# A gated layer in 64-row tiles and two phases in place of full-height tiles

## The chip, the cores and the metric

The kernel runs on one core of a Trainium2 chip. The metric is device time in microseconds (us), lower is better. Five engines work side by side, each on its own queue in program order: PE (matrix multiplies into PSUM banks), ScalarE (ACT), VectorE (DVE), GpSimd (POOL) and SyncE (SP, which issues loads). They wait for one another through semaphores.

## What is computed

Three layers run one after the other: a gated linear attention, an expert layer in which each of 3,072 tokens passes one of eight experts, and a gated layer over all tokens. The change lies in the third, whose reference is:

```python
def _moe2_ref(x, w_gate, w_val, w_out):
    gate = 1.0 / (1.0 + np.exp(-(x @ w_gate)))
    val = x @ w_val
    return (gate * val @ w_out).astype(np.float32)
```

Here x has 3,072 rows and 320 columns, w_gate and w_val are 320 by 1,536, w_out is 1,536 by 320. The weights come in 64 bits. To keep 32-bit accuracy every factor is split in a high and a low part of a shorter format (float32r), and a product is the sum of three: high·high, high·low, low·high.

## The kernel before, in words

The gated layer works on six groups g of 512 tokens and twelve tiles f of 128 hidden columns: 72 steps (g, f), in the order `order2` (line 1451). A step t of the loop at line 1599 does the following.

- `piece_due` and `piece` (lines 1472 and 1465): the weights are loaded in pieces of 320 or 384 columns and split from 64 bits by `f64_split` (line 1060): three DVE operations, an ACT Relu, two or more DVE operations that need it, and an ACT cast. Some pieces are split in the expert layer already, 19 in the first 18 or so steps. `todo` (line 1454) holds each piece with the step at which it is due.
- `gated_l1(t)` (line 1530): PE computes the gate tile g_ps and the value tile v_ps, each 128 hidden columns by 512 tokens in one PSUM bank out of four (0, 1, 2, 6). `l1_tile` (line 916) contracts over 320 rows: two blocks of 128 rows with three products each, then the last 64 rows. For these the tile wgs (or wvs) holds the high part of the weights in rows 0 to 63 and the low part in rows 64 to 127, and x has its last 64 rows twice; so two full-height products are enough, at the price of a fourth product (low·low) that is not needed. In all 8 products for each tile, 16 per step. Then ACT takes the sigmoid of g_ps, DVE multiplies by v_ps, ACT casts the result to the high part hh, POOL subtracts to get the low part hl.
- `gated_l2(t - 2)` (line 1551): the second layer, two steps late. For each of four blocks of 128 tokens three products with w_out (320 columns) into output banks 3, 4, 5 and 7: 12 products. At the end of a group the banks are copied (`gated_keep`, `gated_out`).
- `group_x` (line 1480) on some steps: ACT and POOL split the tokens of the next group.

After the loop the last two steps' second layers are computed block by block (line 1614), each with its output transfer. The program's own order is kept (a manual schedule): what stands here is each engine's queue.

Of the kernel before, what the change touches and what calls it, by code (L numbers as in the profile page):

```python
# [15 lines left out]
ALU = mybir.AluOpType  # L16
# [6 lines left out]
def kernel(  # L23
# [1171 lines left out]
    def flag_ops():  # L1195
# [14 lines left out]
        def of_expert(u):  # L1210
# [23 lines left out]
            lambda: v.tensor_tensor(out=fb, in0=z(0), in1=z(1), op=ALU.add),  # L1234
            total,
# [3 lines left out]
            lambda: v.tensor_tensor(out=z(2), in0=ps[0][:, 0:1], in1=z(2), op=ALU.add),  # L1239
            lambda: v.tensor_scalar_min(z(2), z(2), 1.0),  # L1240
# [171 lines left out]
    for nm in ("wg", "wv"):  # L1412
        glu[nm] = (
            gp.tile([P, 2, F2], F32R, name=nm + "h"),
            gp.tile([P, 2, F2], F32R, name=nm + "l"),
            gp.tile([P, F2], F32R, name=nm + "s"),
        )

    def whole(t):
        return t  # L1420

    def glu_piece(nm, kk, c0, n):
        cs = slice(c0, c0 + n)
        if kk < 2:
            src = (w_gate if nm == "wg" else w_val)[:, cs].bitcast(I32)
            hi, lo, st = glu[nm]
# [3 lines left out]
        halves = [slice(u * RM, (u + 1) * RM) for u in range(2)]  # L1430
# [4 lines left out]
        def parts(u):  # L1435
            return [
                (lambda z, r=r: z[r], glu[m][2][halves[u], cs]) for r, m in zip(halves, ("wg", "wv"))
            ]

        return lambda: f64_split(t, n, parts(0), parts(1))  # L1440

# [81 lines left out]
    todo += [(when[f] + 2, lambda f=f: wo_load(f)) for f in range(NF2)]  # L1523
    todo.sort(key=lambda z: z[0])
# [4 lines left out]

    def gated_l1(t):  # L1530
        g, f = order2[t]
        pg, pv = (next_bank((0, 1, 2, 6), nm) for nm in ("g_ps", "v_ps"))
        l1_tile(pg, glu["wg"], xg[g], f)
        l1_tile(pv, glu["wv"], xg[g], f)
        s = mw.tile([P, NM], F32, tag="sgm", bufs=2, name="sgm")
        nc.scalar.activation(out=s, in_=pg, func=AF.Sigmoid)  # L1536
        nc.vector.tensor_tensor(out=s, in0=pv, in1=s, op=ALU.mult)  # L1537
        gh, gl = ring("hh"), ring("hl")
        nc.scalar.copy(gh, s)  # L1539
        e = nc.gpsimd if t < last else nc.vector  # L1540
        e.tensor_tensor(out=gl, in0=s, in1=gh, op=ALU.subtract)  # L1541
        hs[t] = (gh, gl)

    def begins(t):
        g, f = order2[t]
        return f == 0 or (g < 2 and f == NH)

    def ends_(t):
        return t == last or begins(t + 1)

    def gated_l2(t, js):
# [45 lines left out]
    xsteps.update({order2.index((1, 6)) + 2 * u: (2, u) for u in range(3)})  # L1597
    xsteps.update({order2.index((g, 4 + 2 * u)): (g + 1, u) for g in range(2, NG - 1) for u in range(3)})
    for t in range(NG * NF2):
# [12 lines left out]
        if t in xsteps:  # L1612
            group_x(*xsteps[t])
# [190 lines left out]
    NSB = NE * NTILE  # L1804

    def more_blocks(fp):
        gw = fp.tile([P, NTILE], F32, name="gw")
# [52 lines left out]
        with tc.For_i(0, NE, 1) as e:  # L1860
# [6 lines left out]
            with tc.If(high > low):  # L1867
# [7 lines left out]
                with tc.For_i(low, high, 1) as j:  # L1875
# [36 lines left out]
                    for f in range(NF2):  # L1912
                        pg = mm_ps("fg_ps")[:, 0:P]
                        l1_tile(pg, glu["wg"], (yh, yl), f)
                        pv = mm_ps("fv_ps")[:, 0:P]
                        l1_tile(pv, glu["wv"], (yh, yl), f)
# [71 lines left out]
```

## Time and profile before

| | us |
|---|---|
| median of 3 runs | 773.56 (772.23 to 776.41) |
| the profiled execution's own time | 772.58 |
| its span (first to last instruction) | 770.9 |
| PE busy | 737.4, 96% of the span |
| DVE, ACT, POOL busy | 408.8, 340.0, 393.3 |
| first matmul of the gated layer | 372.3 after the span's start |
| start of its last step | 753.06 |

A matmul group's "busy" is a union of pipelined instructions, whose ends are modelled; what counts is the time from one start to the next. The profile has the granted clock of PE as a share of full speed: 1.00 is 2.4 GHz, 0.50 is 1.2 GHz. "PEld" is PE's weight load. In a row of the timeline "[2.24 <-PE g_ps L926]" says that the engine sat idle 2.24 us before it and what ended that.

### The profile page before, as it was taken

What the parts mean: (1) busy time and instruction counts of PE and PEld (TensorE: products, weight loads), DVE (VectorE), ACT (ScalarE), POOL (GpSimd) and SP (SyncE); (2) the same over time, 40 slices, a digit from 0 to 9 for tenths busy, and PEclk for the clock granted to TensorE, in tenths of its full rate; (3) what the DMA queues carried; (4) which work ended last, traced back from release to release, by engine and by line L of the source; (5) the groups of instructions that cost most, each with busy time, mean ns of one, the idle gap of its engine ahead of it and who ended that gap; (6) DMA issues with size and microseconds to landing.
All of it is one profiled execution on the core that took longest, in us unless ns stands there. A gap on an engine that the chain in (4) does not pass through costs nothing. (4 is left out here: it accounts for less than half of the span.)

```text
span 770.9 us, 13685 instructions
## 1 busy us (share of the span) xinstructions
PE 737.4 (96%) x5013; PEld 667.9 (87%) x5013; DVE 408.8 (53%) x866; ACT 340.0 (44%) x689; POOL 393.3 (51%) x449
## 2 busy tenths in 40 slices
PE   6789998999999999999999999999999999999995
PEld 5689998899878989999888888888888888888885
DVE  7888888878579787855577775121121111111111
ACT  5766554544866655765444343222222222222221
POOL 6677777547676767886242224443334324324222
PEclk9999999599999999999999999999999999999998
DMA  7644765445545566551122221000000000000001
GB/s 224 193 154 148 233 201 153 135 127 150 165 133 157 142 194 180 167 173 58 35 72 80 67 64 34 19 35 0 1 10 27 1 0 35 1 1 34 1 1 38
DMA packets 39846, 70.19 MB, mean 91 GB/s; under 512 B 4818, under 2 KB 28460, under 8 KB 39772
## 3 DMA queue, kind: packets, MB, share of 16 engines
q1 hardware_dynamic: 36764, 59.61, 26.3%
q0 software_dynamic: 3008, 9.64, 3.9%
q8 instruction: 41, 0.67, 0.4%
q14 instruction: 33, 0.27, 0.1%
HBM read 60.55 MB, written 8.68 MB: 90 GB/s over the span
## 5 line engine op out<-in xcount | busy, mean ns | idle before, releaser
L1541 POOL TENSOR_TENSOR hl<-sgm,hh 128x512 fp32r<-128x512 f32 x71 | 91.9, 1294 | 245.1 <-ACT hh L1539 245.1
L1537 DVE TENSOR_TENSOR sgm<-v_ps,sgm 128x512 f32<-128x512 f32 x72 | 49.8, 692 | 244.8 <-PE v_ps L926 244.3
L1539 ACT CAST hh<-sgm 128x512 fp32r<-128x512 f32 x72 | 44.7, 621 | 132.5 <-DVE sgm L1537 132.5
L1536 ACT ACTIVATE sgm<-g_ps 128x512 f32<-128x512 f32 x72 | 42.9, 596 | 109.1 <-PE g_ps L926 109.0
L1561 PE MATMUL o_ps<-wo,hh 128*128 128x320 f32 x288 | 89.0, 309 | 0.0
L1562 PE MATMUL o_ps<-wo,hl 128*128 128x320 f32 x288 | 89.0, 309 | 0.0
L1560 PE MATMUL o_ps<-wo,hh 128*128 128x320 f32 x288 | 88.6, 308 | 0.0
L1014 ACT ACTIVATE hh<-h_ps 128x256 fp32r<-128x256 f32 (+7 forms) x72 | 35.2, 489 | 56.4 <-PE h_ps L926 53.1
L429 PE MATMUL s_ps<-qk 128*128 128x128 f32 (+1 forms) x384 | 52.4, 298 | 6.5 <-DMA qk<-in_qkt_dram 6.5
L1561 PEld LDWEIGHTS o_ps<-wo,hh 128*128 128x128 f32 x288 | 54.0, 188 | 3.1 <-DVE wo L1071 0.4
L1560 PEld LDWEIGHTS o_ps<-wo,hh 128*128 128x128 f32 x288 | 54.1, 188 | 2.7
L1015 DVE SCALAR_TENSOR_TENSOR hl<-h_ps,hh 128x256 fp32r<-128x256 f32 (+7 forms) x72 | 39.5, 551 | 30.9 <-ACT hh L1014 30.5
L429 PEld LDWEIGHTS s_ps<-qk 128*128 128x128 f32 (+1 forms) x384 | 47.7, 206 | 7.6 <-DMA qk<-in_qkt_dram 4.5
L1562 PEld LDWEIGHTS o_ps<-wo,hl 128*128 128x128 f32 x288 | 54.1, 188 | 0.0
L223 POOL TENSOR_TENSOR w1l<-w1raw,w1h 128x512 fp32r<-128x512 f32 x32 | 44.4, 1386 | 14.2 <-ACT w1h L220 12.5
L922 PE MATMUL h_ps<-xh,w1h 128*128 128x256 f32 (+7 forms) x144 | 50.9, 354 | 0.0
L935 PE MATMUL y_ps<-hh,w2h 128*128 128x256 f32 (+7 forms) x144 | 50.0, 347 | 0.0
L936 PE MATMUL y_ps<-hl,w2h 128*128 128x256 f32 (+7 forms) x144 | 48.8, 339 | 0.8 <-DVE hl L1015 0.8
L924 PE MATMUL h_ps<-xh,w1l 128*128 128x256 f32 (+7 forms) x144 | 49.2, 342 | 0.0
L923 PE MATMUL h_ps<-xl,w1h 128*128 128x256 f32 (+7 forms) x144 | 49.1, 341 | 0.0
L234 POOL TENSOR_TENSOR w2l<-w2raw,w2h 128x512 fp32r<-128x512 f32 x28 | 36.8, 1316 | 23.6 <-ACT w2h L232 18.7
L937 PE MATMUL y_ps<-hh,w2l 128*128 128x256 f32 (+7 forms) x144 | 48.7, 338 | 0.0
(337 smaller groups left out, 2081.6 us busy)
## 6 DMA issues: line engine op xcount, KB each, us to landing
kv<-in_kvo_dram SPq DMA_DIRECT2D x24, 484.0 KB
w2raw<-in_moe_w_dram SPq DMA_DIRECT2D x32, 320.0 KB
w1raw<-in_moe_w_dram SPq DMA_DIRECT2D x32, 256.0 KB
qk<-in_qkt_dram SPq DMA_DIRECT2D x48, 160.0 KB
xs<-x SPq DMA_DIRECT2D x24, 192.0 KB
w1raw<-in_moe_w_dram SPq DMA_DIRECT2D x64, 64.0 KB
raw<-in_moe_w_out_dram SPq DMA_DIRECT2D x12, 320.0 KB
raw<-in_moe_w_gate_dram SPq DMA_DIRECT2D x8, 384.0 KB
```

Of the source, the lines that this page charges most:

```text
L429: nc.tensor.matmul(pss[u][:, pr_ * L:(pr_ + 1) * L], qk[i % NQ][rows, 2 * u, pr_, :], qk[i % NQ][rows, 1, pr_, :], start=True, stop=True,)
L922: nc.tensor.matmul(ps, hi[:, kk, fs], h[:, kk], start=(kk == 0), stop=False)
L923: nc.tensor.matmul(ps, hi[:, kk, fs], l[:, kk], start=False, stop=False)
L924: nc.tensor.matmul(ps, lo[:, kk, fs], h[:, kk], start=False, stop=False)
L935: nc.tensor.matmul(ys[d], wh, hh, start=first, stop=False)
L936: nc.tensor.matmul(ys[d], wh, hl, start=False, stop=False)
L937: nc.tensor.matmul(ys[d], wl, hh, start=False, stop=last)
L1537: nc.vector.tensor_tensor(out=s, in0=pv, in1=s, op=ALU.mult)
L1541: e.tensor_tensor(out=gl, in0=s, in1=gh, op=ALU.subtract)
L1560: nc.tensor.matmul(o, gh[:, ts_], wh, start=begins(t), stop=False)
L1561: nc.tensor.matmul(o, gh[:, ts_], wl, start=False, stop=False)
L1562: nc.tensor.matmul(o, gl[:, ts_], wh, start=False, stop=ends_(t))
```

## The change

All products of the gated layer are cut into 64-row halves; PE addresses the rows 0 to 63 and the rows 64 to 127 as two tiles, with weights of their own, and a product of one half and one of the other are issued in turn.

- The first layer is in two phases. `gated_a`: the three products of the last 64 rows (the tiles wth and wtl hold the gate's in rows 0 to 63 and the value's in rows 64 to 127), then for both 128-row blocks the lower half of the rows into g_ps and the upper half into v_ps. `gated_b`: the lower half into v_ps and the upper into g_ps.
- The second layer (`gated_l2h`) has two phases in the same way: in the first the lower half of hh and hl goes into one output bank and the upper half into its neighbour, in the second the other way round.
- The two halves are kept from writing one bank at the same time: `note` has ACT write one element after a phase's last product, and `turn_rows` has the next phase's first product wait for that write.
- A step is now: phase one of the first layer, phase one of the second layer of step t-2, phase two of the first, phase two of the second. A piece's split is cut in three: its middle stands before phase two, its casts behind it, its first DVE operations after the step's DVE product.
- Phase one of steps 0 and 1 and a whole piece (the first of w_out) come before phase two of step 0. Pieces are due one step earlier.
- The last 64 rows' pieces need one cast and one DVE operation less each. In the last step the operations between the layers are cut in two column halves. The one-column product of the flags is issued together with its reader.

```diff
-    todo = [(when[z[2] // P], lambda z=z: glu_piece(*z)) for z in todo]
+    todo = [(when[z[2] // P] - 1, lambda z=z: glu_piece(*z)) for z in todo]
...
+    def products(rows, ps, w, x, kk, fs, start=False, stop=False):
+        (wh, wl), (h, l) = w, x
+        at = lambda z: z[rows, kk, fs] if len(z.shape) == 3 else z[rows, fs]
+        return [
+            lambda: nc.tensor.matmul(ps, at(wh), h[rows, kk], start=start, stop=False),
+            lambda: nc.tensor.matmul(ps, at(wh), l[rows, kk], start=False, stop=False),
+            lambda: nc.tensor.matmul(ps, at(wl), h[rows, kk], start=False, stop=stop),
+        ]
...
+    def note(ins, key):
+
+        passed[key] = nc.scalar.copy(seen, zeros[0:1, 0:1])
+        tc.add_manual_dep(passed[key].ins, ins.ins.name, sync, reason="these products are done")
+
+    def turn_rows(ins, key):
+
+        tc.add_manual_dep(ins.ins, passed.pop(key).ins.name, sync, reason="the other rows wrote the bank")
+
-    def gated_l1(t):
+    def gated_a(t):
         g, f = order2[t]
-        pg, pv = (next_bank((0, 1, 2, 6), nm) for nm in ("g_ps", "v_ps"))
-        l1_tile(pg, glu["wg"], xg[g], f)
-        l1_tile(pv, glu["wv"], xg[g], f)
+        fs = slice(f * P, (f + 1) * P)
+        gv[t] = [next_bank((0, 1, 2, 6), nm) for nm in ("g_ps", "v_ps")]
+        weave(*(products(r, ps, tails, xg[g], 2, fs, start=True) for r, ps in zip(halves, gv[t])))
+        for kk in range(2):
+            ins = woven(*(products(r, ps, w, xg[g], kk, fs) for r, ps, w in zip(halves, gv[t], gate_val)))
+        note(ins[-1], "l1")
+
+    def gated_b(t):
+        g, f = order2[t]
+        fs = slice(f * P, (f + 1) * P)
+        for kk in range(2):
+            ins = woven(*(
+                products(r, ps, w, xg[g], kk, fs, stop=(kk == 1))
+                for r, ps, w in zip(halves, gv[t][::-1], gate_val[::-1])
+            ))
+            if kk == 0 and "l1" in passed:
+                turn_rows(ins[0], "l1")
...
+    def gated_l2h(t, phase):
...
+        for j in (0, 2):
+            ins = woven(*(three(halves[u], j + (u ^ swap)) for u in range(2)))
+            if phase and j == 0:
+                turn_rows(ins[0], "l2")
+        if not phase:
+            note(ins[-1], "l2")
...
     for t in range(NG * NF2):
-        g, f = order2[t]
         piece_due(t)
-        gated_l1(t)
+        if t == 0:
+            gated_a(0)
+            gated_a(1)
+            for ops in piece():
+                weave(ops)
         if t >= 2:
-            gated_l2(t - 2, allj)
+            gated_a(t)
+            gated_l2h(t - 2, 0)
+        weave(rest[0])
+        weave(rest[1])
+        s = gated_b(t)
+        if t >= 2:
+            gated_l2h(t - 2, 1)
             if ends_(t - 2):
                 g2, f2 = order2[t - 2]
                 (gated_out(g2, allj) if f2 == NF2 - 1 else gated_keep(g2))
-        weave(defer[0:2], *piece())
+        weave(rest[2])
+        a, *rest = piece()
+        weave(a)
+        gated_h(t, s)
+        weave(defer[0:2])
```

How the order moves. First PE's queue in a step. Before, the end of the first layer and the first two blocks of the second (g_ps, v_ps: gate and value; o_ps: output banks; wo: w_out; waits on an engine's semaphore in brackets):

```order
L925 MATMUL v_ps<-xg,wvs 128x512
L926 MATMUL v_ps<-xg,wvs 128x512
L1560 MATMUL o_ps<-wo,hh 128x320 [waits Activation_49]
L1561 MATMUL o_ps<-wo,hh 128x320 [waits DVE_49]
L1562 MATMUL o_ps<-wo,hl 128x320 [waits Pool_49]
L1560 MATMUL o_ps<-wo,hh 128x320
```

Now, the end of phase one, phase one of the second layer (two blocks of tokens in each run of rows marked x2) and the start of phase two:

```order
L1533 MATMUL g_ps<-xg,wgl 128x512
L1533 MATMUL v_ps<-xg,wvl 128x512
L1609 MATMUL o_ps<-wo,hh 128x320 x2
L1610 MATMUL o_ps<-wo,hh 128x320 x2
L1611 MATMUL o_ps<-wo,hl 128x320 [waits Pool_49]
L1611 MATMUL o_ps<-wo,hl 128x320
L1609 MATMUL o_ps<-wo,hh 128x320 x2
L1610 MATMUL o_ps<-wo,hh 128x320 x2
L1611 MATMUL o_ps<-wo,hl 128x320 x2
L1531 MATMUL v_ps<-xg,wvh 128x512 [waits Activation_49]
L1531 MATMUL g_ps<-xg,wgh 128x512
```

The second layer, which was one run of 12 products behind the first, now stands in two halves, and the first of them lies between the two phases of the first layer. Phase two begins with a wait for ACT.

Second, ACT's queue from the end of the expert layer on. Before (sgm: the sigmoid's tile; fa and fb: a piece's; wo: a piece of w_out; xh: tokens of the next group):

```order
L968 COPY yT_3227<-y_ps_5075 128x336 [waits Pool_49]
L1536 ACT_TABLE_LOAD
L1536 ACTIVATE sgm_5265<-g_ps_5247 128x512 [waits PE_49]
L1539 CAST hh_5268<-sgm_5265 128x512 [waits DVE_49]
L1085 ACTIVATE fa_5272<-fa_5272,relu_b_2322 128x320 [waits DVE_49]
L1068 CAST wo_5239<-fb_5273 128x320 [waits DVE_49]
L1536 ACTIVATE sgm_5303<-g_ps_5285 128x512 [waits PE_49,Activation_49]
L1539 CAST hh_5306<-sgm_5303 128x512 [waits DVE_49]
L1085 ACTIVATE fa_5310<-fa_5310,relu_b_2322 128x320 [waits DVE_49]
L1068 CAST wo_5239<-fb_5311 128x320 [waits DVE_49]
L209 CAST xh_5323<-yT_3227 128x512 [waits Activation_49]
```

Now, from the write that follows phase one of step 1:

```order
L1545 COPY seen_5243<-zeros_94 1x1 [waits PE_49,Activation_49]
L1085 ACTIVATE fa_5286<-fa_5286,relu_b_2322 128x320 [waits DVE_49]
L1068 CAST wo_5235<-fb_5287 128x320 [waits DVE_49]
L1574 ACT_TABLE_LOAD
L1574 ACTIVATE sgm_5311<-g_ps_5244 128x512 [waits PE_49]
L1585 CAST hh_5320<-sgm_5311 128x512 [waits DVE_49]
L1085 ACTIVATE fa_5314<-fa_5314,relu_b_2322 128x320 [waits DVE_49]
L1574 ACTIVATE sgm_5342<-g_ps_5265 128x512 [waits PE_49]
L1068 CAST wo_5235<-fb_5315 128x320 [waits DVE_49]
L1585 CAST hh_5352<-sgm_5342 128x512 [waits DVE_49]
L209 CAST xh_5356<-yT_3227 128x512
L1545 COPY seen_5243<-zeros_94 1x1 [waits PE_49,Activation_49] x2
```

The writes into `seen` come ahead of everything else; the first piece's Relu and cast moved ahead of the table load and of the first sigmoid, and the writes for step 2 (the last row) stand behind two steps' sigmoids and casts and a cast of tokens.

## Rows read from the trace of the kernel before

**Rows 1.** Stage table: stretch, each engine's busy us, clock, DMA share, GB/s.

```profile
379.60:500.00 120.40, 120.35 (x623) 105.60 (x622) 74.39 (x144) 49.74 (x95) 42.04 (x33) 1.00 0.20 56
```

**Rows 2.** Timeline, two steps of the gated layer, PE: start us, us, engine.

```profile
520.43 0.39 PE L922 MATMUL g_ps<-xg,wgh 128*128 128x512 f32 x1
520.43 0.19 PEld L923 LDWEIGHTS g_ps<-xg,wgh 128*128 128x128 f32 x1
523.85 0.39 PE L926 MATMUL v_ps<-xg,wvs 128*128 128x512 f32 x1
524.08 0.30 PE L1560 MATMUL o_ps<-wo,hh 128*128 128x320 f32 x1
525.83 0.39 PE L922 MATMUL g_ps<-xg,wgh 128*128 128x512 f32 x1
```

**Rows 3.** The same timeline, ScalarE and VectorE in that step.

```profile
522.52 0.60 ACT L1536 ACTIVATE sgm<-g_ps 128x512 f32<-128x512 f32 x1 [2.24 <-PE g_ps L926]
524.35 0.69 DVE L1537 TENSOR_TENSOR sgm<-v_ps,sgm 128x512 f32<-128x512 f32 x1 [4.44 <-PE v_ps L926]
525.07 0.62 ACT L1539 CAST hh<-sgm 128x512 fp32r<-128x512 f32 x1 [1.95 <-DVE sgm L1537]
```

**Rows 4.** Timeline of the first score products, 40 rows each, then full-height ones.

```profile
4.97 0.58 PE L429 MATMUL s_ps<-qk 40*128 40x128 f32 x2 [0.31 <-DMA qk<-in_qkt_dram]
4.97 0.29 PEld L429 LDWEIGHTS s_ps<-qk 40*128 40x128 f32 x2 [0.60 <-DMA qk<-in_qkt_dram]
4.97 2.07 PE L429 MATMUL s_ps<-qk 40*128 40x128 f32 x14 [0.31 <-DMA qk<-in_qkt_dram]
10.84 3.48 PE L429 MATMUL s_ps<-qk 128*128 128x128 f32 x15 [2.28 <-DMA qk<-in_qkt_dram]
```

**Rows 5.** Groups of instructions, ScalarE, whole span: count, busy us, mean ns.

```profile
L1397 ACT ACTIVATE dum<-zeros 128x1 f32<-128x1 f32 x1 | 0.2, 203 | 0.0
L209 ACT CAST xh<-yT 128x512 fp32r<-128x512 f32 x9 | 5.5, 616 | 0.0
```

**Rows 6.** Timeline, start of the gated layer, and one later piece (446.55).

```profile
372.29 0.39 PE L922 MATMUL g_ps<-xg,wgh 128*128 128x512 f32 x1
373.40 1.28 ACT L1536 ACT_TABLE_LOAD   x1
377.46 0.56 ACT L1085 ACTIVATE fa<-fa,relu_b 128x320 int32<-128x320 int32 x1
377.63 1.29 POOL L1541 TENSOR_TENSOR hl<-sgm,hh 128x512 fp32r<-128x512 f32 x1 [10.88 <-ACT hh L1539]
378.05 1.22 DVE L1086 SCALAR_TENSOR_TENSOR fb<-raw,fa 128x320 int32<-128x320 int32 x1 [0.92 <-ACT fa L1085]
379.30 0.46 ACT L1068 CAST wo<-fb 128x320 fp32r<-128x320 f32 x1 [1.28 <-DVE fb L1086]
380.18 0.49 DVE L1071 SCALAR_TENSOR_TENSOR wo<-fc,fa 128x320 fp32r<-128x320 int32 x1
446.55 0.56 DVE L1086 SCALAR_TENSOR_TENSOR fb<-raw,fa 128x384 int32<-128x384 int32 x1 [0.68 <-ACT fa L1085]
```

**Rows 7.** Timeline, a ScalarE result that PE's weight load waits for.

```profile
20.25 0.62 ACT L483 ACTIVATE cst<-u_ps 40x164 f32<-40x164 f32 x2
20.92 0.20 PEld L476 LDWEIGHTS u_ps<-vw,kv 128*40 128x40 f32 x6 [0.96 <-ACT cst L483]
```

**Rows 8.** Stage table: two stretches with little PE work, and those behind them.

```profile
31.20:34.60 3.40, 2.19 (x30) 1.98 (x31) 2.79 (x9) 2.95 (x9) 3.27 (x7) 1.00 0.83 224
34.60:38.00 3.40, 3.40 (x19) 3.40 (x18) 3.15 (x4) 1.97 (x7) 1.88 (x2) 0.50 0.96 308
133.60:137.00 3.40, 1.11 (x7) 0.60 (x7) 2.66 (x5) 1.19 (x3) 2.02 (x4) 1.00 0.97 302
137.00:157.50 20.50, 20.06 (x139) 19.66 (x139) 15.51 (x45) 10.96 (x30) 12.30 (x16) 0.50 0.45 134
```

**Rows 9.** Timeline, the last step's subtraction on VectorE.

```profile
758.36 0.69 DVE L1541 TENSOR_TENSOR hl<-sgm,hh 128x512 fp32r<-128x512 f32 x1 [0.69 <-ACT hh L1539]
```

More of the change, by code (lines that the diff above doesn't have):

```diff
@@ L1238, in flag_ops @@
             ),
[L1239 removed]
+            lambda: (total(), v.tensor_tensor(out=z(2), in0=ps[0][:, 0:1], in1=z(2), op=ALU.add)),
             lambda: v.tensor_scalar_min(z(2), z(2), 1.0),
@@ L1415 @@
             gp.tile([P, 2, F2], F32R, name=nm + "l"),
-            gp.tile([P, F2], F32R, name=nm + "s"),
         )
+    tails = [gp.tile([P, F2], F32R, name="wt" + v) for v in "hl"]
     def whole(t):
         return t
+    halves = [slice(u * RM, (u + 1) * RM) for u in range(2)]
     def glu_piece(nm, kk, c0, n):
@@ L1425, in glu_piece @@
             src = (w_gate if nm == "wg" else w_val)[:, cs].bitcast(I32)
-            hi, lo, st = glu[nm]
+            hi, lo = glu[nm]
             t = f64_load([(slice(0, P), src[kk * P:(kk + 1) * P])], n)
             return lambda: f64_split(t, n, [(whole, hi[:, kk, cs])], [(whole, lo[:, kk, cs])])
-        halves = [slice(u * RM, (u + 1) * RM) for u in range(2)]
         t = f64_load(
@@ L1433, in glu_piece @@
         )
[L1435 to L1440, printed above, removed]
+        return lambda: f64_split(t, n, [(whole, tails[0][:, cs])], [(whole, tails[1][:, cs])])
     todo = sorted(
@@ L1522 @@
     load_wo()
-    todo += [(when[f] + 2, lambda f=f: wo_load(f)) for f in range(NF2)]
+    todo += [(when[f] + 1, lambda f=f: wo_load(f)) for f in range(NF2)]
     todo.sort(key=lambda z: z[0])
@@ L1528 @@
     hs, os_ = {}, {}
-    def gated_l1(t):
-        g, f = order2[t]
-        pg, pv = (next_bank((0, 1, 2, 6), nm) for nm in ("g_ps", "v_ps"))
-        l1_tile(pg, glu["wg"], xg[g], f)
-        l1_tile(pv, glu["wv"], xg[g], f)
-        s = mw.tile([P, NM], F32, tag="sgm", bufs=2, name="sgm")
-        nc.scalar.activation(out=s, in_=pg, func=AF.Sigmoid)
-        nc.vector.tensor_tensor(out=s, in0=pv, in1=s, op=ALU.mult)
+    gv = {}
+    gate_val = (glu["wg"], glu["wv"])
+    def products(rows, ps, w, x, kk, fs, start=False, stop=False):
[6 more added lines that the diff above has]
+        ]
@@ new lines, with woven @@
+    seen = const.tile([1, 1], F32, name="seen")
+    sync = mybir.DependencyInfo(mybir.DependencyClass.Sync, mybir.DependencyReason.DATA)
+    passed = {}
+    def woven(*chains):
+        return [op() for ops in zip(*chains) for op in ops]
+    def note(ins, key):
[3 more added lines that the diff above has]
+        tc.add_manual_dep(ins.ins, passed.pop(key).ins.name, sync, reason="the other rows wrote the bank")
@@ new lines, in gated_a @@
+    def gated_a(t):
+        g, f = order2[t]
+        fs = slice(f * P, (f + 1) * P)
[14 more added lines that the diff above has]
+                turn_rows(ins[0], "l1")
+        pg, pv = gv.pop(t)
+        s = mw.tile([P, NM], F32, tag="sgm", bufs=2, name="sgm")
+        for cs in col_parts(t):
+            nc.scalar.activation(out=s[:, cs], in_=pg[:, cs], func=AF.Sigmoid)
+            nc.vector.tensor_tensor(out=s[:, cs], in0=pv[:, cs], in1=s[:, cs], op=ALU.mult)
+        return s
@@ L1538, in gated_l1, with col_parts, gated_h @@
+    def col_parts(t):
+        return [slice(0, NM)] if t < last else [slice(u * NM // 2, (u + 1) * NM // 2) for u in range(2)]
+    def gated_h(t, s):
         gh, gl = ring("hh"), ring("hl")
-        nc.scalar.copy(gh, s)
         e = nc.gpsimd if t < last else nc.vector
-        e.tensor_tensor(out=gl, in0=s, in1=gh, op=ALU.subtract)
+        for cs in col_parts(t):
+            nc.scalar.copy(gh[:, cs], s[:, cs])
+            e.tensor_tensor(out=gl[:, cs], in0=s[:, cs], in1=gh[:, cs], op=ALU.subtract)
@@ L1549, in ends_, with three @@
         return t == last or begins(t + 1)
+    def gated_l2h(t, phase):
+        g, f = order2[t]
+        swap = (f + phase) % 2
+        begin, end = begins(t) and phase == 0, ends_(t) and phase == 1
+        if begin:
+            os_[g] = [bank(j, "o_ps") for j in (3, 4, 5, 7)]
+        gh, gl = hs[t]
+        wh, wl = wo[f]
+        def three(rows, j):
+            o = os_[g][j][:, 0:DM]
+            ts_ = slice(j * P, (j + 1) * P)
+            return [
+                lambda: nc.tensor.matmul(o, gh[rows, ts_], wh[rows], start=begin, stop=False),
+                lambda: nc.tensor.matmul(o, gh[rows, ts_], wl[rows], start=False, stop=False),
+                lambda: nc.tensor.matmul(o, gl[rows, ts_], wh[rows], start=False, stop=end),
+            ]
+        for j in (0, 2):
[4 more added lines that the diff above has]
+            note(ins[-1], "l2")
     def gated_l2(t, js):
@@ L1598 @@
     xsteps.update({order2.index((g, 4 + 2 * u)): (g + 1, u) for g in range(2, NG - 1) for u in range(3)})
+    rest = ([],) * 3
     for t in range(NG * NF2):
-        g, f = order2[t]
         piece_due(t)
-        gated_l1(t)
-        if t >= 2:
-            gated_l2(t - 2, allj)
+        if t == 0:
[3 more added lines that the diff above has]
+                weave(ops)
+        if t >= 2:
+            gated_a(t)
[5 more added lines that the diff above has]
+            gated_l2h(t - 2, 1)
             if ends_(t - 2):
@@ L1804, with l1_any @@
     NSB = NE * NTILE
+    def l1_any(ps, u, x, f):
+        fs = slice(f * P, (f + 1) * P)
+        for rows, w, kk in (
+            (slice(0, P), gate_val[u], 0), (slice(0, P), gate_val[u], 1), (halves[u], tails, 2)
+        ):
+            weave(products(rows, ps, w, x, kk, fs, start=(kk == 0), stop=(kk == 2)))
     def more_blocks(fp):
```

5 lines of the change are left out of this document (2 added, 3 removed).

## The prediction

> **What bounds the kernel now.** I read the stage table first. In the gated layer the matrix engine (PE) is busy 120.35 of 120.40 us [rows 1], so this phase is worth exactly what PE's own work in it is worth. Next, the timeline of one step: its first matmul starts at 520.43, the next step's at 525.83, a period of 5.40 us [rows 2]. The 16 products of 512 columns fill 520.43 to 524.08, 0.228 us each (I use 0.227, the pitch inside the run), and the 12 of 320 columns fill 524.08 to 525.83, 0.146 us each. The difference, 0.081 us for 192 columns, is 2.4 columns per ns; so 512 columns stream in 0.213 us, 320 in 0.133, and every matmul carries a fixed 13 ns besides. The weight load of the next matmul starts with the matmul before it and lasts 0.19 us [rows 2]: it is hidden. The other engines' work of a step is a chain of 0.60, 0.69, 0.62 and 1.29 us [rows 3, 6], far below 5.40, and PE never waits for it. The page's chain of what ended last holds only the final output transfer and says nothing of this phase.
>
> **What the change removes.** The 64 tail rows of the contraction cost each of the two tiles g and v two full-height products (hi and lo of the weights stacked in one tile): 4 slots of 512 per step. They become three products of 64 rows each for g and v, and g's and v's run side by side, one in each half of the rows: 3 slots. All other products are cut in two 64-row halves, which also run side by side, so their slots stay: 12 of 512 and 12 of 320. Per step 15 slots of 512 in place of 16: one slot of 0.227 us, over 72 steps **−16.3 us**. This rests on two claims.
>
> First, do halves run at the same time? The trace has 64-row tiles in one place: the first 16 score products, 40 rows each in alternate halves. A pair of them takes 0.58 us together, and its two weight loads 0.29 [rows 4]: partners start side by side, within 0.01 us as the row can tell. Fourteen of them take 2.07 us, while 15 full-height ones of the same 128 columns soon after take 3.48 [rows 4]. Less 0.58 us for one, that is 0.115 us for each further half product against 0.207 for a full one, though not all of the fourteen met a partner. So they overlap, loads included.
>
> Second, what does a pair cost at 512 and 320 columns? Fixed rest and partners' offset decide. No row shows it at these sizes. Best case: the partners hide each other's 13 ns, the pair is 0.213. Worst case with overlap: each pays its own, 0.240. I take one rest per pair, 0.227 and 0.146, because the pairs of [rows 4] show no pitch of their own beside that of full-height products. The Trainium skill has a rule that speaks against this change. In "TensorEngine Tiling (Array Packing)", Performance Considerations, each matmul has an overhead of about 60 cycles; an estimate from it, 25 ns at 2.4 GHz for each of the 26 matmuls added to 28, is 0.65 us per step or +47 us, against +0 by my sum. The 13 ns of [rows 2] disagree with it as a price in a stream.
>
> **What it adds.** Two one-element ScalarE (ACT) writes per step, 0.20 us each [rows 5], each waited for by PE. In the steady step let e be the end of phase two of the first layer. PE then has 6 slots of 320 (to e+0.88), phase one of the next step (9 slots, e+2.92) and 6 slots of 320 (e+3.80) before it needs the first write. A result reaches another engine 0.27 us after its slot (matmul at 523.85, slot over at 524.08, VectorE (DVE) at 524.35 [rows 2, 3]); ACT's writes reach PE's load within 0.05 us (20.87 to 20.92 [rows 7]), and I allow 0.10. So the write may run e+3.19 to e+3.39 and PE may go on at e+3.49, 0.31 us early: nothing is lost, the cover being the 0.88 us of output products. ACT must be free at e+3.19; sigmoid, DVE's product and the cast end by e+2.25, with a group's cast of 0.62 by e+2.87. The second write has phase two, 1.36 us, as cover. Behind a late write ACT's next sigmoid is queued, and DVE's product and GpSimd (POOL) behind that; none is near its limit.
>
> In the first 18 steps DVE also splits weight pieces, now cut in three parts around the step. The long operation of a piece took 1.22 us while POOL subtracted, and 0.56 when POOL was idle (446.55) [rows 6]. Now it comes after POOL's subtraction, so it gets shorter; DVE's product is late by some 0.1 us and the cover holds. I charge 0.6 us for small waits here and at the copies of output banks, which PE now needs sooner after they were filled.
>
> **The start is where it loses.** All of ACT's queue stands behind the two first writes (order, above). By hand, from the durations of [rows 3, 5, 6]: PE starts at 372.29; phase one of steps 0 and 1 is 18 slots, to 376.37. The second write runs 376.64 to 376.84 and PE goes on at 376.94: 0.6 us lost, with nothing between to cover it. Only now come the piece's Relu (to 377.40), DVE's long operation (378.0), the cast (378.5), the table load of 1.28 (379.8), sigmoid (380.4) and DVE's product (381.1). PE has finished both phases two at 379.7, and phase one of step 2 needs the bank that this product reads: 1.5 us lost. Then cast, Relu, sigmoid of step 1 (382.9), DVE's piece, held up by POOL until 383.4, its product (384.9), cast and the group's cast (386.2) stand ahead of the write that step 2 waits for: it ends at 386.4, PE was through at 384.1: 2.4 us lost. Sum **+4.5 us**. Before, the table load ran at 373.40 to 374.68, hidden.
>
> **The clock.** After stretches in which PE was busy 2.19 of 3.40 us and 1.11 of 3.40 us the granted clock was 0.50 for 3.4 and for 20.5 us [rows 8]. From 379.7 to 386.5 PE would be busy 2.9 of 6.8 us, so I expect one such fall. Half speed for 3.4 us loses 1.7, for 20.5 us 10.2. I take **+1.7**, as the row with the shorter fall had PE busy all through, as here.
>
> **The end.** The last step's chain, split in column halves, is covered by 6+3 slots of 320 where it had 12+3. With halves it takes about 1.5 us (half an activation, product and cast, each near 0.4) after a cover of 1.3: +0.4; before, the subtraction began at 758.36 [rows 9] under running products. Dropped tail copies and the moved one-column product lie beside PE's work: 0. SP has only the piece loads, due a step later: 0.
>
> Sum: −16.3 + 4.5 + 0.6 + 1.7 + 0.4 = −9.1. The profiled execution took 772.6 us; that gives **763.5**. The median shown, 773.56, is 1.0 above that execution. About 0.5% (3.9 us) is what a measurement can tell from no change.
>
> **The rivals.**
> *A rest per matmul (slower).* If the 13 ns belong to an engine-wide step, each of the 54 matmuls pays them: 27 × 13.3 ns × 72 = +25.9, **789.4**. It decides from 4.7 ns per pair on (9.1 us over 1,944 pairs). For it: the rest is there at both sizes. Against: the pairs of [rows 4]. Chance 0.11.
> *The partners' offset adds up (no change).* The two of [rows 4] bound it by 10 ns; at half that, 5 ns × 1,944 = +9.7, **773.2**. The Trainium skill's page "TensorE: Matmul & The Clock Gate", Part 3 (Packing small matmuls), gives about 4 ns per further tile; by it the estimate is +7.8, 771.3. Chance 0.10.
> *The rest is hidden in the pair.* −25.9, **737.6**; half of it 750.5. For it: two loads overlapped fully. Chance 0.12.
> *Overlap fails at full speed.* The pairs of [rows 4] ran at 0.21 us per 128 columns, slow ones. If none overlaps, 5.16 us per step more, 1,135. The same Part 3 of the Trainium skill states a speedup of 3.07 for four tiles; an estimate with that share of the ideal is a pair 1.3 times as long, some 110 us more. Chance 0.04.
> *The waits are dearer.* The write's cover fails by 0.1 us in each step (+7), or the clock stays low for 20 us (+8.5): **771**. Chance 0.06.
>
> **How the numbers follow.** My case, 0.57, spans 757 to 771: start loss 2 to 6, clock 0 to 10. With the offset case, the dearer waits and the better half of the hidden rest down to 749, and up to 779, about 0.78 is held. Faster: 0.53 of my case and 0.12, so 0.65; same: 0.04, 0.10 and 0.03, so 0.17; slower 0.18.
>
> **What would show it.** Right: a steady step of 5.16 to 5.20 us; partners starting within 0.01 us; next pair 0.227 and 0.146 later; no wait of PE for the one-element writes after step 3; three waits near 377, 380 and 385 us, the granted clock perhaps at 0.50 behind them. Wrong: pair pitches other than these, a wait on the write in every step, a table load that hides, or PE idle for long at the last step.

## The result, and the profile after

The changed kernel takes 767.39 us (median of 7 runs, 764.88 to 769.53) against 773.75 for the kernel before in the same comparison: a ratio of 0.991, 95% interval 0.990 to 0.9925. The forecast was 763.5, faster; the time lies 3.9 us above it, inside the range of 757 to 771.

The profiled execution took 767.39 us, its span is 765.6 (before: 772.6 and 770.9). From the first product of the gated layer to the span's end it is 391.7 us where it was 398.6: 6.9 us gained. Ahead of the gated layer, where the change does no more than shorten the splitting of some weight pieces, this execution is 1.6 us longer (the first product starts at 373.87, before at 372.29 [rows 6]). Its first spell of half clock lasts 6.8 us where that of [rows 8] lasts 3.4, which is the likely reason; no run isolates it.

The stage table of the changed kernel (stretch, its length, then busy us and instructions of PE, PEld, DVE, ACT and POOL, then clock, DMA share, GB/s). First the stretch of that spell, then two of the gated layer:

```profile
31.20:34.60 3.40, 2.11 (x9) 1.78 (x9) 2.87 (x9) 2.95 (x9) 3.27 (x6) 0.62 0.92 301
379.60:500.00 120.40, 117.83 (x1200) 101.45 (x1198) 66.88 (x142) 57.59 (x138) 44.67 (x33) 1.00 0.20 57
500.00:620.00 120.00, 120.00 (x1237) 104.22 (x1235) 25.43 (x56) 40.57 (x100) 45.08 (x37) 1.00 0.03 12
```

PE is still the bound; the 2.6 us in which it idles in the second stretch ([rows 1] had 0.05) are the start of the layer. Its timeline, PE, ScalarE and VectorE (start, us, engine):

```profile
378.69 0.50 PE L1531 MATMUL v_ps<-xg,wvh 64*128 64x512 f32 x1 [0.34 <-ACT seen L1545]
380.14 1.28 ACT L1574 ACT_TABLE_LOAD   x1
382.06 0.69 DVE L1575 TENSOR_TENSOR sgm<-v_ps,sgm 128x512 f32<-128x512 f32 x1 [1.55 <-ACT sgm L1574]
382.08 0.50 PE L1531 MATMUL g_ps<-xg,wth 64*128 64x512 f32 x1 [0.33 <-ACT sgm L1574]
382.81 0.49 PE L1531 MATMUL v_ps<-xg,wth 64*128 64x512 f32 x1 [0.23 <-DVE sgm L1575]
386.78 0.62 ACT L1585 CAST hh<-sgm 128x512 fp32r<-128x512 f32 x1 [1.03 <-DVE sgm L1575]
387.82 0.41 ACT L1545 COPY seen<-zeros 1x1 f32<-1x1 f32 x2
388.06 0.50 PE L1531 MATMUL v_ps<-xg,wvh 64*128 64x512 f32 x1 [2.01 <-ACT seen L1545]
390.44 0.39 PE L1531 MATMUL g_ps<-xg,wth 64*128 64x512 f32 x1
```

These are the three waits of the forecast, each with the releaser it named: the write behind step 1 (378.69), sigmoid and product behind the table load (382.08, 382.81), the writes behind the cast of step 1 (388.06). Step 3 begins at 390.44, 16.57 us after the first product. In the kernel before it began here, 12.66 us after the first product:

```profile
384.95 0.39 PE L922 MATMUL g_ps<-xg,wgh 128*128 128x512 f32 x1
```

With the 0.5 us that the three steps save in slots, the start loses 4.4 us.

A step in the middle, PE and ScalarE of the changed kernel:

```profile
521.72 0.39 PE L1531 MATMUL g_ps<-xg,wth 64*128 64x512 f32 x1
521.72 0.39 PE L1531 MATMUL v_ps<-xg,wth 64*128 64x512 f32 x1
523.81 0.31 PE L1609 MATMUL o_ps<-wo,hh 64*128 64x320 f32 x2
524.07 0.19 ACT L1545 COPY seen<-zeros 1x1 f32<-1x1 f32 x1 [0.98 <-PE v_ps L1533]
524.69 0.39 PE L1531 MATMUL v_ps<-xg,wvh 64*128 64x512 f32 x1
526.09 0.30 PE L1609 MATMUL o_ps<-wo,hh 64*128 64x320 f32 x2
526.96 0.39 PE L1531 MATMUL g_ps<-xg,wth 64*128 64x512 f32 x1
```

Partners start together. The period is 5.24 us (526.96 less 521.72), where it was 5.40 to 5.41 [rows 2] and 5.16 to 5.20 was forecast. The 12 pairs of 320 columns take 0.88 and 0.87 us, as full products did. But the nine pairs of 512 columns take 2.09 (521.72 to 523.81), the six 1.40: 0.233 us a pair, not 0.227. The write ends at 524.26; PE goes on at 524.69, right behind the products of w_out, and has not waited.

### The profile page after: what moved, and what is told of

Read it like the earlier page. It is cut to its first block, busy times and chain, and to the rows that moved or that the text cites. A ratio compares the mean times of both kernels' runs of the same rounds, so it can differ in the third digit from the quotient of the medians.

```text
span 765.6 us, 17594 instructions
## 1 busy us (share of the span) xinstructions
PE 730.9 (95%) x6861; PEld 656.2 (86%) x6861; DVE 402.4 (53%) x864; ACT 363.9 (48%) x829; POOL 395.5 (52%) x449
## 5 line engine op out<-in xcount | busy, mean ns | idle before, releaser
L1611 PE MATMUL o_ps<-wo,hl 64*128 64x320 f32 x560 | 87.2, 307 | 0.0
L1610 PE MATMUL o_ps<-wo,hh 64*128 64x320 f32 x560 | 86.7, 305 | 0.0
L1609 PE MATMUL o_ps<-wo,hh 64*128 64x320 f32 x560 | 86.3, 303 | 0.0
L1531 PE MATMUL v_ps<-xg,wvh 64*128 64x512 f32 x144 | 56.5, 392 | 2.4 <-ACT seen L1545 2.4
L1609 PEld LDWEIGHTS o_ps<-wo,hh 64*128 64x128 f32 x560 | 53.0, 185 | 6.3
L1610 PEld LDWEIGHTS o_ps<-wo,hh 64*128 64x128 f32 x560 | 52.8, 184 | 5.8
L1531 PE MATMUL g_ps<-xg,wgh 64*128 64x512 f32 x144 | 56.5, 392 | 0.0
L1532 PE MATMUL v_ps<-xg,wvh 64*128 64x512 f32 x144 | 56.4, 392 | 0.0
L1532 PE MATMUL g_ps<-xg,wgh 64*128 64x512 f32 x144 | 56.4, 392 | 0.0
L1532 PE MATMUL g_ps<-xl,wgh 64*128 64x512 f32 x144 | 56.4, 392 | 0.0
L1532 PE MATMUL v_ps<-xl,wvh 64*128 64x512 f32 x144 | 56.4, 392 | 0.0
L1531 PE MATMUL g_ps<-xh,wgh 64*128 64x512 f32 x144 | 56.3, 391 | 0.0
L1531 PE MATMUL v_ps<-xh,wvh 64*128 64x512 f32 x144 | 56.3, 391 | 0.0
L1533 PE MATMUL g_ps<-xg,wgl 64*128 64x512 f32 x144 | 56.2, 390 | 0.0
```

Of the source, the lines that this page charges most:

```text
L1531: lambda: nc.tensor.matmul(ps, at(wh), h[rows, kk], start=start, stop=False),
L1532: lambda: nc.tensor.matmul(ps, at(wh), l[rows, kk], start=False, stop=False),
L1533: lambda: nc.tensor.matmul(ps, at(wl), h[rows, kk], start=False, stop=stop),
L1609: lambda: nc.tensor.matmul(o, gh[rows, ts_], wh[rows], start=begin, stop=False),
L1610: lambda: nc.tensor.matmul(o, gh[rows, ts_], wl[rows], start=False, stop=False),
L1611: lambda: nc.tensor.matmul(o, gl[rows, ts_], wh[rows], start=False, stop=end),
```

## Experiments

A ratio is that of a run's time to the kernel before, measured beside it. A step, or the gated layer's part (from its first product to the span's end), is read from the run's trace. A slot is the time from the start of one product, or pair, to the start of the next; a turn is a change between full-height products and halves.

**1. Only the tail in halves.** The order of before, 12 full products, then three pairs:

```
for ps, w in zip(pss, gate_val):
    for kk in range(2):
        weave(products(slice(0, P), ps, w, xg[g], kk, fs, start=(kk == 0)))
weave(*(products(r, ps, tails, xg[g], 2, fs, stop=True) for r, ps in zip(halves, pss)))
```

> Only the tail rows are done in halves: 3 pairs of 64-row products for g and v together; the other 12 products of 512 columns and the 12 of 320 are full-height again, in the order of the kernel before, without phases and without the one-element writes. A step is then 12 x 226.7 + 3 x 233 + 12 x 146.7 ns = 5.18 us, if going from full products to halves and back costs nothing. Theory: each such turn costs 0.20 us. In the trace of the changed kernel the slot before the first pair of the gated layer lasts 0.247 in place of 0.153 us and that pair's own 0.340 in place of 0.233; at the end, where full products follow halves, 0.239 and 0.253 in place of 0.147 each. Two turns a step, 72 steps: +28.8 us, about 788 us, a step of 5.58. Rival: those stretched slots are waits of that place, and a turn in the middle of a stream is free: 759 us, a step of 5.18 to 5.20, and the phases and writes of the change were not needed.

Measured: 790.13 us, ratio 1.021 (1.019 to 1.023), a step of 5.64. Its timeline at the two turns, PE:

```profile
525.39 0.39 PE L1533 MATMUL v_ps<-xg,wvl 128*128 128x512 f32 x1
525.72 0.50 PE L1531 MATMUL g_ps<-xg,wth 64*128 64x512 f32 x1
526.06 0.39 PE L1532 MATMUL g_ps<-xg,wth 64*128 64x512 f32 x1
526.29 0.39 PE L1533 MATMUL g_ps<-xg,wtl 64*128 64x512 f32 x1
526.62 0.42 PE L1619 MATMUL o_ps<-wo,hh 128*128 128x320 f32 x1
526.87 0.31 PE L1620 MATMUL o_ps<-wo,hh 128*128 128x320 f32 x1
```

Into the pairs the slots last 0.33 and 0.34 us in place of 0.233, out of them 0.33 and 0.25 in place of 0.233 and 0.147: 0.20 us a turn, 0.40 a step. The two turns are dearer than the one slot that three pairs save, so the tail alone in halves does not pay. The Trainium skill's "TensorEngine Tiling (Array Packing)", Key Properties, says that a change of the tiling mode drains the engine. The trace agrees in so far as a turn costs 0.20 us; that this time is a drain, it does not show.

**2. The start.** A table load ahead of time, and step 0's own write:

```
+    nc.scalar.activation(out=dum, in_=zeros[:, 0:1], func=AF.Sigmoid)
     weave(last_part)
...
-        note(ins[-1], "l1")
+        note(ins[-1], ("l1", t))
...
-            if kk == 0 and "l1" in passed:
-                turn_rows(ins[0], "l1")
+            if kk == 0:
+                turn_rows(ins[0], ("l1", t))
```

> The changed kernel with two edits at the start of the gated layer: a one-column Sigmoid on ScalarE ahead of the last copies of the expert layer brings the table load forward, and phase two of step 0 waits for the write behind step 0's own phase one, not for the one behind step 1's. Theory: the first wait (0.6 us) goes, and the first sigmoid comes 1.3 us earlier, so that the second wait shrinks from 1.1 to about 0.5; the third (2.0 us) ends 1.2 us earlier and is then the longest, 2.4 us: 1.2 us less in all, about 766.2 against 767.4. Rival: the writes for step 2 wait for VectorE's piece, not for the sigmoid's chain, so nothing moves at the third wait: 767.4, the same within 0.3 us.

Measured: 766.65 us, ratio 0.992 (0.990 to 0.993): no difference from the change that the times can tell, and in the trace the gated layer's part is 391.66 us against 391.70. PE's waits there (line, releaser: us in all, times, longest), and the stretch behind the wait in the stage table:

```profile
PE v_ps L1532 <- ACT seen L1546: 2.0, 1, 2.0
385.00:388.40 3.40, 3.30 (x18) 2.73 (x20) 2.28 (x3) 0.97 (x4) 2.41 (x2) 0.51 0.28 84
```

The first two waits are gone and the third is 2.0 us, but behind it the granted clock was 0.51 for 3.4 us. From the end of that wait to step 3 it takes 3.90 us (385.10 to 389.00), in the changed kernel 2.38 (388.06 to 390.44): the clock takes back 1.5 us. This is the fall that the forecast put at 1.7; the changed kernel's own profile has the same wait and no fall.

**3. Full products in the new order.** Undoes the halves, keeps phases, writes and pieces:

```
-        weave(*(products(r, ps, tails, xg[g], 2, fs, start=True) for r, ps in zip(halves, gv[t])))
...
+        for ps in gv[t]:
+            nc.tensor.matmul(ps, tails[0][:, fs], h[:, 2], start=True, stop=False)
+            nc.tensor.matmul(ps, tails[0][:, fs], l[:, 2], start=False, stop=False)
...
-            ins = woven(*(products(r, ps, w, xg[g], kk, fs) for r, ps, w in zip(halves, gv[t], gate_val)))
+        ins = woven(*(products(slice(0, P), ps, w, xg[g], 0, fs) for ps, w in zip(gv[t], gate_val)))
...
```

> The order of the change, its phases, its writes and its pieces, but every product full-height and alone: 16 slots of 512 and 12 of 320 a step. The tail products multiply the stacked tail rows of both tiles, so the output isn't the reference's. Theory: what the change lost against its sum lies in the pairs, not in the order: a step of 5.39 to 5.43 us as before, and only the start's 4 to 5 us and the end's 0.4 on top: about 779 to 780 us. Rival: two phases and the writes cost time of their own in every step, and the pairs gain more than was seen: a step of 5.48 or more, 784 us and up.

Measured: 783.31 us, ratio 1.013 (1.011 to 1.015), a step of 5.48: the rival's step. But its reason, a price of phases and writes, is not what shows. In its timeline a full product of 512 columns takes 0.233 us as well:

```profile
521.84 0.39 PE L1558 MATMUL g_ps<-xg,wth 128*128 128x512 f32 x1
523.94 0.39 PE L1533 MATMUL v_ps<-xg,wvl 128*128 128x512 f32 x1
```

Nine slots in 2.10 us. So the 0.233 is not a price of pairs. Against this kernel the halves gain what the forecast said: 5.48 less 5.24 is 0.24 us a step, one slot.

**4. The pitch of pairs by size.** Longer runs of pairs, fewer columns in three groups:

```
+    COLS = (512, 512, 384, 256, 320, 512)
...
-        for kk in range(2):
+        for kk in (0, 1) * 3:
...
```

> The changed kernel with the products of the first layer beyond the tail repeated three times (runs of 21 and 18 pairs), and with 384 columns in group 2, 256 in group 3 and 320 in group 4 in place of 512; the rest of each gated tile is filled with zeros. The output isn't the reference's; what is read is the steady pitch of a pair at each size. Full-height products keep 13.3 ns beside their columns at 512, 384, 336 and 320 columns. Theory: a pair keeps 20 ns at every size: 233.3 at 512, 180.0 at 384, 153.3 at 320, 126.7 at 256. Rival 1: what is added grows with the columns (the mean slots of 232.5 at 512 and 145.8 at 320 give 0.4516 ns a column and 1.3 fixed): 174.7 at 384, 116.9 at 256, 145.8 at 320. Rival 2: only the longest products pay: 233.3 at 512, but 173.3, 146.7 and 120.0 below.

Measured, the first and the last product of one run of 21 pairs each, at 512, 384, 320 and 256 columns:

```profile
521.21 0.39 PE L1532 MATMUL g_ps<-xg,wth 64*128 64x512 f32 x1
525.88 0.39 PE L1534 MATMUL g_ps<-xg,wgl 64*128 64x512 f32 x1
638.13 0.33 PE L1532 MATMUL g_ps<-xg,wth 64*128 64x384 f32 x1
641.60 0.33 PE L1534 MATMUL g_ps<-xg,wgl 64*128 64x384 f32 x1
853.02 0.31 PE L1532 MATMUL g_ps<-xg,wth 64*128 64x320 f32 x1
855.96 0.31 PE L1534 MATMUL g_ps<-xg,wgl 64*128 64x320 f32 x1
751.09 0.28 PE L1532 MATMUL g_ps<-xh,wth 64*128 64x256 f32 x1
753.44 0.28 PE L1534 MATMUL g_ps<-xh,wgl 64*128 64x256 f32 x1
```

Divided by 20: 233.5, 173.5, 147 and 117.5 ns. Beside their columns at 2.4 a nanosecond that is 20, 13.5, 13.7 and 11. Rival 2 holds, roughly: only the longest products pay more, and at 256 columns pairs even keep less than 13 ns. A rest of 20 ns that every pair keeps is excluded.

What experiments 1, 3 and 4 share with the changed kernel is its memory map: the new tile `seen` (four bytes, 32 in the map) moves the pools of the tokens, of w_out and of the gated tiles up by 32 bytes, while the gate and value weights, kept at the other end of the memory, stay. The bytes are those of the program's memory map; no trace shows addresses. The theory that the rest of the runs test is that this shift makes the 512-column products slow. The rivals are the order of the products and the new tile in itself.

**5. No new tile.** `seen = dum[0:1, 0:1]` in place of `const.tile([1, 1], F32, name="seen")`.

> The changed kernel with one edit: the one-element writes go into the first element of a column that the kernel has already, so that no new tile is made. The new tile had moved all tiles of the two pools that hold the tokens (xg, xh, xl), w_out and the gated tiles by 32 bytes (the first xg from byte 68064 of a partition to 68096), while the gate and value weights stayed (167904). New theory: that shift is what slows the 512-column products, halves or full, from 226.7 to 233.3 ns; full products in the new order showed 233.4 too, and so did those with only the tail in halves. Then pairs go at 226.7 but for the first slots behind a run of 320, the step falls from 5.24 to 5.15 to 5.18 us, and the time by 4.5 to 6.5 us: 761 to 763 us. Rival: it is the order of the products (no full tail products in the middle of a tile), or the pairs themselves: nothing moves, step 5.24, 767 us.

Measured: 764.97 us, ratio 0.990 (0.987 to 0.993); the step is 5.20, the gated layer's part 388.83 us against 391.70. The gain of 2.9 us is less than the 4.5 to 6.5 expected. From its timeline, g's half of the first, sixth and ninth pair of phase one, and of the next step's first:

```profile
521.21 0.39 PE L1531 MATMUL g_ps<-xg,wth 64*128 64x512 f32 x1
522.37 0.39 PE L1533 MATMUL g_ps<-xg,wgl 64*128 64x512 f32 x1
523.05 0.39 PE L1533 MATMUL g_ps<-xg,wgl 64*128 64x512 f32 x1
526.41 0.39 PE L1531 MATMUL g_ps<-xg,wth 64*128 64x512 f32 x1
```

The first five pairs behind a run of 320 columns take 1.16 us (521.21 to 522.37), 0.232 each; the later ones 0.226 to 0.227. In nanoseconds the slots are 231, 236, 228, 233, 231, then 227, within one nanosecond those of full products in the kernel before. With two runs of 512 in a step these slower five come twice, and cost more than the expectation had allowed.

**6. The kernel before with the shift alone.** `pad = const.tile([1, 1], F32, name="pad")`, filled once by GpSimd, never read.

> The kernel before with one more tile of four bytes, which takes 32: the tokens, w_out and gated tiles move by 32 bytes as in the change, and nothing else is changed (one small write of GpSimd at the start of the gated layer fills the tile). Theory of the shift: all 16 products of 512 columns of a step take 231 to 235 ns in place of five of them, the step goes from 5.41 to 5.48 us: 5 to 6 us slower, about 779 us. Rival: the place of the tiles means nothing, 773.5 us.

Measured: 778.74 us, ratio 1.007 (1.005 to 1.010), a step of 5.49. The first three steps of the gated layer hold 48 products of 512 columns in a row; the first of them and the product behind the last:

```profile
370.94 0.39 PE L922 MATMUL g_ps<-xg,wgh 128*128 128x512 f32 x1
382.13 0.30 PE L1562 MATMUL o_ps<-wo,hh 128*128 128x320 f32 x1
```

11.19 us, 0.233 each. In the kernel before the same 48 took 10.90, 0.227, from 372.29 [rows 6] to the product behind them:

```profile
383.19 0.30 PE L1560 MATMUL o_ps<-wo,hh 128*128 128x320 f32 x1
```

A tile that nothing reads costs this kernel 6 us.

**7. The weights moved too.** The changed kernel with `seen`, and 224 bytes of filling behind the weights in their pool:

```
     tails = [gp.tile([P, F2], F32R, name="wt" + v) for v in "hl"]
+    fill = gp.tile([P, 56], F32, name="fill")
+    nc.gpsimd.memset(fill, 0.0)
```

> The changed kernel with its new tile left in place, and 224 bytes of filling behind the gate and value weights (written once, never read), so that these move by 224 bytes too: from the first xg (68096) to the first weight (167680) it is again a multiple of 256 bytes, as in the kernel before (68064 to 167904), where the change made it 32 less. Theory: the distance between what streams and what is loaded decides, so the 512-column pairs fall back to the pattern of before (231, 236, 228, 233, 231, then 227), the step to 5.20, the time to about 765. Rival: it is the place of the token tiles alone (68096 against 68064): pairs at 233, step 5.24, 767.

Measured: 763.18 us, ratio 0.987 (0.985 to 0.9895), a step of 5.20 with the slots of run 5. From its timeline, the start of a step, the product behind its nine pairs, and the start of the next step:

```profile
522.35 0.39 PE L1533 MATMUL g_ps<-xg,wth 64*128 64x512 f32 x1
524.41 0.31 PE L1611 MATMUL o_ps<-wo,hh 64*128 64x320 f32 x2
527.55 0.39 PE L1533 MATMUL g_ps<-xg,wth 64*128 64x512 f32 x1
```

The nine pairs take 2.06 us where the changed kernel's took 2.09. The tokens lie where the change put them and the new tile is there, yet the pairs are fast: neither the place of the tokens nor the tile in itself decides, but how tokens and weights lie to one another. That it is their distance is the simplest reading; a kernel in which the weights alone are moved was not run.

**8 and 9. Other shifts**, by a `seen` of 9 and of 25 elements.

> The changed kernel with a tile of 36 bytes for the writes, which takes 64: the shift is 64 bytes in place of 32. If the distance between the tokens and the weights decides, the pitch of the 512-column pairs may come out at 226.7 ns (about 762 us), at 233 (767) or at another value, but it moves with the shift; which one the theory can't say. Rival: any new tile does the same, 233 and 767 us.

> The changed kernel with a tile for the writes that takes 128 bytes, so that the distance is a multiple of 128 but not of 256. If the pattern of the distance repeats every 128 bytes or less: pairs as with no shift, step 5.20. Rival: it repeats at 256 or more: another pitch, step 5.21 to 5.26. The shifts of 32 and 64 bytes gave 5.24 and 5.21.

Measured: 765.38 us (ratio 0.9895, 0.986 to 0.993) with a step of 5.21, and 768.46 in a single run with a step of 5.25. The pairs take 231 to 232 ns on the mean at 64 bytes, 232 to 233 at 128, each in a pattern of its own. Of the four distances only the multiple of 256 bytes had a run of 227; why that is so, no run here shows.

**10. Four writes for one.** Three more `nc.scalar.copy(seen, ...)` in `note`, PE waits for the last.

> The changed kernel with four one-element writes in place of each one; PE waits for the last. Theory (the cover of the prediction): the write between the two layers' first phases ends 0.43 us before phase two begins (524.26 against 524.69), 0.35 of it to spare; three more writes take 0.6 us, so each step loses 0.25 and the whole 18 us: 785 us; the second layer's write has 0.9 us to spare and costs nothing. Rival 1: the writes cost PE their time in every step already: 0.6 or 1.2 us a step, 810 us or more. Rival 2: there is more room than the trace shows, 767 us.

Measured: 795.27 us, ratio 1.029 (1.026 to 1.031), a step of 5.63: 0.39 more, not 0.25. From its timeline, ScalarE's last three writes and PE:

```profile
520.39 0.64 ACT L1548 COPY seen<-zeros 1x1 f32<-1x1 f32 x3
520.65 0.31 PE L1613 MATMUL o_ps<-wo,hl 64*128 64x320 f32 x2
521.08 0.50 PE L1531 MATMUL v_ps<-xg,wvh 64*128 64x512 f32 x1
521.42 0.39 PE L1532 MATMUL v_ps<-xg,wvh 64*128 64x512 f32 x1
```

The cover is real: 0.67 us more of writing open a hole of 0.29 (520.79, where the last product of w_out leaves off, to 521.08), so 0.38 were to spare; the writes reach PE 0.05 us after their end. Missed was what a hole costs besides: the first slot behind it takes 0.34 us in place of 0.233, 0.11 more. 0.39 us over 72 steps are the 28 us.

**11. The piece later.** The first piece of w_out behind step 0's cast, in place of ahead of its product.

```
-            for ops in piece():
-                weave(ops)
...
+        if t == 0:
+            gated_h(t, s)
+            for ops in piece():
+                weave(ops)
         a, *rest = piece()
...
```

> The changed kernel with the first piece of w_out split behind step 0's sigmoid, product and cast, not ahead of them. Theory: the table load and the first sigmoid come 1.5 us earlier, so that the second wait of the start (1.1 us) goes; but PE's first product of w_out then waits for this piece, and the writes for step 2 stand behind it: the start loses as much as before, the gated layer's part of the span 391 to 393 us against 391.7. Rival 1: the piece ahead is what delays the start, and without it 1.5 us are gained: 390.2. Rival 2: the product of w_out waits long: 394 or more.

Measured: 769.62 us in a single run, the gated layer's part 395.0 us. PE's waits at the start:

```profile
PE v_ps L1531 <- ACT seen L1545: 3.6, 2, 3.3
PE o_ps L1609 <- ACT wo L1068: 0.6, 1, 0.6
```

The second wait goes, as expected; but PE waits for the piece (0.6) and, for the writes behind it, 3.3 us in place of 2.0. From 386.0, inside that wait, to 392.9 the clock was at half: from the wait's end to step 3 it takes 4.32 us in place of 2.38, so 1.9 of the 395.0 are the clock's. Without them 393.0 is left, the theory's upper end; 395.0 falls to rival 2 by number, but the wait for the piece is short. The piece ahead is not what makes the start slow.

**12. All that helped together.** No new tile, the earlier table load, step 0's own write, and no piece between steps 0 and 1:

```
-        a, *rest = piece()
+        if t == 6:
+            gated_h(t, s)
+            for ops in piece():
+                weave(ops)
+        a, *rest = piece() if t else ([],) * 4
...
```

> The writes into the existing column, the earlier table load and step 0's own write (as in the run on the start), and one thing more: no piece is split between the products of steps 0 and 1; it comes a step later, and one is caught up in step 6. Expected: 5 us from the shift, 1 from the first two waits, and 2.0 from the third, since ScalarE then has only a cast of tokens between step 1's cast and the writes for step 2: about 758 to 760 us. Rival: the third wait only moves to the piece that is caught up or to the products of w_out: 761 to 762.

Measured: 760.77 us, ratio 0.985 (0.982 to 0.988), the gated layer's part 386.59. From its timeline at the start, and its one long wait later on:

```profile
371.43 0.39 PE L1534 MATMUL g_ps<-xg,wgl 64*128 64x512 f32 x1
376.87 0.39 PE L1534 MATMUL g_ps<-xg,wgl 64*128 64x512 f32 x1
377.58 0.49 PE L1532 MATMUL v_ps<-xg,wth 64*128 64x512 f32 x1
380.73 0.49 PE L1532 MATMUL v_ps<-xg,wvh 64*128 64x512 f32 x1
408.00 0.50 PE L1532 MATMUL v_ps<-xh,wvh 64*128 64x512 f32 x1 [1.00 <-ACT dum L1546]
```

From 371.43 to 376.87, 24 pairs follow one another at 0.227 us across two steps. Of the second wait something is left: at 377.58 the value tile's half starts 0.48 us behind its partner. The third wait is gone (380.73 follows the products of w_out, which leave off at 380.64), and the clock stays up. The piece that is caught up in step 6 costs 1.3 us at 408, so the rival holds in part, and the time is 0.8 us above the expected 758 to 760. This version beats both kernels.

## Why the prediction was right, and where it was off

Faster, by the mechanism named, but the profiled execution gained 5.2 us in place of 9.1. That it came so near is in part luck: the slot was missed by 4.3 us, and the fall of the clock, put at 1.7, did not come in this execution. By the forecast's own steps:

| step | forecast, us | measured, us |
|---|---|---|
| one slot of 512 a step, 72 steps | -16.3 | -12.0 (5.407 to 5.240 a step) |
| start | +4.5 | +4.4 |
| small waits | +0.6 | +0.2 (0.6, where the kernel before had 0.4) |
| the clock at the start | +1.7 | 0 in this profile, 1.5 in that of run 2 |
| end | +0.4 | +0.6 (18.2 from the last step's start to the span's end; before 17.8, less the slot saved 17.6) |
| ahead of the gated layer | 0 | +1.6, likely of the longer spell of half clock |

*Halves run at the same time*: right. Partners start 3 to 4 ns apart in the changed kernel, and a pair takes what a full product takes (runs 3 and 5). In about half of run 7's pairs they start 16 to 17 ns apart, and its step is 5.20 all the same: the offset is not added to the slot. The rivals of a rest per matmul, of an offset that adds up, of a rest hidden in the pair and of overlap that fails are out: with the shift taken away, pairs and full products have the same slots within one nanosecond. The overhead of about 60 cycles a matmul in the Trainium skill's "TensorEngine Tiling (Array Packing)", Performance Considerations, would be by estimate 25 ns for each matmul added; no run shows it: the changed kernel has 54 matmuls a step where run 3 has 28, and its step is 0.24 us shorter, one slot. The 4 ns a tile of the Trainium skill's "TensorE: Matmul & The Clock Gate", Part 3, are there between partners, but a stream of pairs does not pay them.

*A pair costs 0.227 us*: this is the step that failed. It took the slot from inside a run of the kernel before and held that it would stay; 0.233 was measured, which the forecast had named as a sign of being wrong, and a step of 5.24 lies outside its 5.16 to 5.20. The pairs are not the reason. Of the 4.3 us, 2.9 are the shift of 32 bytes that the new tile brings (5.240 against 5.200 a step in runs 5 and 7); run 6 shows the same shift slow the kernel before. The other 1.4 are the second run of 512 columns in each step: the first five slots behind a run of 320 take 26 ns more in all, and the change made one such place into two (5.200 against the 5.18 that one slot less would give). Some of it comes back in the first slots of 320 columns, 143 and 145 ns for 147. The trace of before had the mark of this: 0.228 on the mean of a step beside 0.227 inside the run [rows 2], and the prediction took the smaller without asking where the rest was. Nor is a rest of 13 ns common to all products there: in the expert layer those of 416 to 480 columns have slots of 190 to 217 ns, some 16 beside their columns.

*The start*: right in place, releaser and size. The waits cost 0.6, 1.3 and 2.3 us against 0.6, 1.5 and 2.4, each with the slower first slot behind it; of the 1.3, some 0.2 are that the gate's half then runs a slot ahead of the value's. Run 2 shows that the table load and the wait for step 1's write are behind the first two; run 12 against run 2, that the piece split between steps 0 and 1 is behind the third. The turns between full products and halves, which the forecast put at nothing, take 0.1 us of the start and 0.2 of the end.

*The clock*: right as a risk. Of the nine kernels here with a third wait of 2.0 us or more, six show half clock for 3.4 to 6.8 us across its end or just behind it (runs 2 and 7 to 11), three don't (the changed kernel, runs 3 and 5); what decides between them, no run shows. Run 12, without the wait, shows none.

*No wait for the writes in the steady step*: right, and run 10 gives the cover as 0.38 us where 0.31 was worked out.

## What to carry to other kernels

Before cutting products into halves, see what stands next to them: a turn between full and half rows cost 0.20 us here, so the tail alone in halves, with two turns a step, lost 17 us where all in halves gained 6. After an edit that adds a tile, however small, compare the pitch of unchanged instructions first; here a four-byte tile moved the tokens that stream against the weights that are loaded: 6 us of the kernel before, 3 of the changed one, without showing in any wait. A wait of the bounding engine is to be priced with its first slot behind it and with the clock, not by its idle time alone.

## What was not expected of the hardware

The slot of a 512-column product depends here on how the tile that streams and the weights lie to one another in memory. On the mean of a step's 15 pairs it was 230 ns where their distance was a multiple of 256 bytes (runs 5 and 7), 231 at 64 bytes off, 232 to 233 at 128 and at 32; slots of 227 one behind the other came only with the multiple. Products of 320 columns, whose two tiles moved together, kept to 145 to 146 on the mean. And a change of size leaves a mark: the first five 512-column slots behind shorter products take 228 to 236 ns even at the good distance, while the same products behind other 512-column ones take 227. Both effects are in the traces; what in the engine does it stays open.
